# Soft-capped attention and MLP: first loads by two queues, weight pieces behind the sums

## The chip, the cores and the metric

The kernel runs on one core of one Trainium2 chip. The metric is the device time of one execution in microseconds (us); of several executions the median counts.

## What is computed

Four batches of twelve heads of attention over 448 positions of 64 numbers, with scores that are soft-capped, and then an MLP whose first layer is a relu that is squared:

```python
scores = scale * np.matmul(q, k.transpose(0, 1, 3, 2))      # (4, 12, 448, 448)
scores = cap * np.tanh(scores / cap)
attn = np.exp(scores - scores.max(-1, keepdims=True))
attn = attn / (attn.sum(-1, keepdims=True) + 1e-09)
x = np.matmul(attn, v).transpose(0, 2, 1, 3).reshape(1792, 768)
h = np.maximum(x @ w_in, 0.0)                               # w_in 768 x 2048, float64
return (h * h @ w_out).astype(np.float32)                   # w_out 2048 x 768, float64
```

## The kernel before

The 48 heads are worked on as 24 pairs. A loop over n (its passes are called cycles here, 0 to 24) writes the program of all engines by hand: the order of the code is the order on each engine and on each queue. In cycle n the engines do this:

- TensorE computes the scores of pair n in three units (L407), pv of pair n - 1 (L449, L459) and the sums of its exponentials (`sums`, L466). Every second cycle it also computes the half-scores that two pairs share (L416). ScalarE does tanh (L425) and exp (L433).
- VectorE turns the loaded k and q of a later pair (`turn_kq`, L399), adds the exponentials (L437, L440), and takes pv and sums out of PSUM (`evac`, L471).
- The sums go a long way round. SyncE moves them from `e` or `u` into 64 rows, `cmp` (L474, two transfers of 3.5 KB a pair, at the end of cycle n for pair n - 1). VectorE takes the reciprocal two cycles later (`invert`, L478), SyncE writes it to DRAM as `rd` (L480), GpSimd spreads it over the partitions (`spread`, L488, the cycle after), and VectorE multiplies (`normalise`, L502). In the last cycles these steps follow each other more closely: cycle 23 holds the reciprocal and the spread of pair 20.
- The loads of k (GpSimd) and q (SyncE) come in pieces of 32 partitions, four of each a pair (`load_part`, L368), v in two (L385, GpSimd).

During attention four columns of w_in are fetched as float64, in 24 pieces of 128 KB (`fetch_early`, L578, SyncE). The table `FETCH` (L587) gives for each piece the cycle in which it is issued. Six pieces make a column; ScalarE and VectorE decode columns 0, 1 and 2 in the cycles that the tables `SCALAR` and `VECTOR` name. For column 2 ScalarE starts in cycle 19 (L40).

At the start `NWARM` matmuls of zeros run on TensorE (L528). The first pair's k and q come by several queues, the transposes of k and of q follow on VectorE, and behind them the reciprocal of cap, which ScalarE loads into a register before the first tanh (L541 to L544). `issue_after` gives the scheduler a place in the order for the loads of pair 1.

Behind the loop the first MLP layer begins on TensorE (L357); its order comes from a planner. Its operands hold the normalised outputs of all pairs (`xt`, L786).

Of the kernel before, what the change touches and what calls it, by code (L numbers as in the profile page):

```python
# [240 lines left out]
def tile_softcap_attention_mlp(ctx, tc, q, k, v, cap, w_in, w_out, out):  # L241
    nc = tc.nc
# [10 lines left out]
    NF = DFF // P  # L253
    HO = DM // 2
    scale = 1.0 / float(D) ** 0.5
    NWARM = 14
    NKQ = 3
    NKV = 3
    NEXTRA = 5
# [56 lines left out]
    def prepare():  # L316

        nc.vector.memset(ones, 1.0)
        for t in vn:
            nc.vector.memset(t[:, ::NS + 2], 1.0)  # L320
# [3 lines left out]
    def new_raw(pool, bufs):  # L324
        return pool.tile([P, DM], U64, tag="wraw", name="wraw", bufs=bufs)
# [4 lines left out]
    def w_rows(f):  # L330

        return w_in[:, f * P:(f + 1) * P].rearrange("(c h p) f -> h p c f", h=2, p=D)
# [31 lines left out]
    def load_part(n, i, a, queue):  # L364
        b, j = divmod(n, NPAIR)
        w = a % 2
        x = (k, q)[i][b, 2 * j + head(n, a // 2), :, 32 * w:32 * w + 32].rearrange("(t r) e -> r t e", r=32)
        queue.dma_start(out=kqn[n % NKQ][32 * a:32 * a + 32, i], in_=x)  # L368

    def load_kq(n, i, *queues):  # L370
        for a in range(4):
            load_part(n, i, a, queues[a % len(queues)])
# [7 lines left out]
    def load_v(n):  # L380

        b, j = divmod(n, NPAIR)
        x = v[b, 2 * j:2 * j + 2].rearrange("h (t r) d -> (h t) r d", r=D)
        for i, r in enumerate((bottom, top)):
            nc.gpsimd.dma_start(out=vn[n % NKV][r, 1 + i:1 + i + NS], in_=x[i::2].rearrange("t r d -> r t d"))  # L385

    def new_u():
        return ep.tile([P, 2, S], F32, tag="u", name="u", bufs=3)

    NU = 4  # L390
    last = {}
    kqs, ps, probs, adds, pvs, es, rds, by = {}, {}, {}, {}, {}, {}, {}, {}


    def turn_kq(n, parts=1):
        kqs[n] = qp.tile([P, 2 * S], F32, tag="kq", name="kq")
        src, w = kqn[n % NKQ].rearrange("p i t e -> p (i t e)"), 2 * S // parts
        for i in range(parts):
            done = nc.vector.transpose(out=kqs[n][:, i * w:(i + 1) * w], in_=src[:, i * w:(i + 1) * w])  # L399
            last.setdefault("turn", done)  # L400

    def scores(n, u):
        sc = ps_s.tile([P, 2, 512], F32, tag="s", name="sc")
        kt, qt = kqs[n][:, :S], kqs[n][:, S:]
        for i, r in enumerate((top, bottom)):
            h = head(n, i)
            nc.tensor.matmul(out=sc[:, h, :S], lhsT=kt[r, keys(h, u)], rhs=qt[r], start=True, stop=True)  # L407
        probs[n, u] = sc
# [10 lines left out]
    def tanh(n, u):  # L419
        if u in (1, 3):  # L420
            c = 2 if u == 3 and n % 2 else 4
            ps[n, u // 3] = pp.tile([P, c, S], F32, tag=f"p{c}{u}", name="p", bufs=2 if c == 4 else 1)
        at = 2 * (u in (2, 0))
        p = ps[n, int(u not in (1, 2))][:, at:at + 2]
        nc.scalar.activation(out=p, in_=probs[n, u][:, :, :S], func=ACTF.Tanh, scale=by["qks"])  # L425
        if u:
            probs[n, u] = p
        else:
            probs[n, 0], probs[n + 1, 0] = p[:, 0], p[:, 1]

    def exp(n, i):
        p = ps.pop((n, i))
        nc.scalar.activation(out=p, in_=p, func=ACTF.Exp, scale=by["cap"])  # L433

    def add_p(n):
        adds[n] = pp.tile([P, 2, S], F32, tag="add", name="add")
        nc.vector.tensor_add(out=adds[n], in0=probs[n, 1], in1=probs[n, 2])  # L437
# [31 lines left out]
    def evac(n):  # L469
        e = es[n] = new_u() if n % 4 else keep.tile([P, 2, S], F32, tag="e", name="e")  # L470
        nc.vector.tensor_tensor(out=e, in0=pvs.pop(n)[:, :, :S], in1=guard.unsqueeze(2).to_broadcast([P, 2, S]), op=ALU.add)  # L471
        rds[n] = ep.tile([NC, HB], F32, tag="cmp", name="cmp", bufs=NE)
        for h in range(2):
            nc.sync.dma_start(out=rds[n][h * NC // 2:(h + 1) * NC // 2], in_=e[D * h:D * h + D:32, h])  # L474

    def invert(n):
        cmp = rds[n]
        nc.vector.reciprocal(out=cmp, in_=cmp)  # L478
        rd = dram.tile([2, 2, 2, HS], F32, tag="rd", name="rd", bufs=NE)
        nc.sync.dma_start(out=rd.rearrange("h r c (o e) -> (h r c o) e", e=HB), in_=cmp)  # L480
        rds[n] = rd
# [44 lines left out]
    warm = ps_s.tile([P, 2, 512], F32, tag="s", name="warm")[:, 0]  # L526
    for _ in range(NWARM):
        nc.tensor.matmul(out=warm[:, :P], lhsT=zero, rhs=zero, start=True, stop=True)  # L528
    load_kq(0, 0, nc.sync, nc.scalar)
    load_kq(0, 1, nc.sync, nc.scalar, nc.gpsimd, nc.gpsimd)  # L530
    nc.gpsimd.dma_start(out=cap_sb, in_=cap.partition_broadcast(P))
    nc.scalar.activation(out=guard[:, 0:1], in_=zero[:, 0:1], func=ACTF.Tanh)
    prepare()
    turn_kq(0, 2)
    with tc.issue_after(last["turn"].ins):
        load_kq(1, 0, nc.gpsimd)
        load_kq(1, 1, nc.sync)
    load_v(0)
    load_kq(2, 0, nc.gpsimd)
    load_kq(2, 1, nc.sync)  # L540
# [5 lines left out]
    def prepare_cap():  # L546

        nc.vector.tensor_scalar_mul(ncap, cap_sb, -1.0)
        nc.vector.tensor_tensor(out=ncap, in0=ncap, in1=cap_sb, op=ALU.min)
        nc.vector.tensor_scalar(out=far, in0=ncap[0:1], scalar1=-CAP_MAX, scalar2=None, op0=ALU.is_lt)  # L550

        nc.scalar.activation(out=guard[:, 0:1], in_=ncap, func=ACTF.Exp)
# [18 lines left out]
    def fetch_early(n):  # L571

        for i in [i for i, at in enumerate(FETCH) if at == n]:
            f, c = i // 6, i % 6 // 2 * 2
            if i % 6 == 0:
                raws[f] = new_raw(scr, 2)
            h, r = i % 2, rows[i % 2]
            nc.sync.dma_start(out=raws[f][r, c * P:(c + 2) * P].rearrange("p (c f) -> p c f", f=P),  # L578
                              in_=w_rows(f)[h, :, c:c + 2])
# [4 lines left out]
    HB = 28  # L584
    NC = 4 * S // HB
    DEEP = 3
    FETCH = 3, 4, 5, 6, 7, 7, 8, 9, 10, 11, 12, 13, 15, 15, 16, 16, 17, 18, 21, 21, 22, 22, 23, 23  # L587
    SCALAR = {9: (0, "size"), 11: (0, "rest"), 15: (1, "size"), 17: (1, "rest"), 19: (2, "size"), 21: (2, "rest")}
    VECTOR = {10: ((0, "clip"), (0, "shift")), 12: ((0, "sign"),), 14: ((0, "total"),), 16: ((0, "high0"), (0, "low0")),
              18: ((0, "high1"), (0, "low1"), (1, "clip"), (1, "shift")), 19: ((1, "sign"),),  # L590
# [17 lines left out]
    for n in range(NP + 1):  # L608
        on, prep, old = n < NP, n + 1 < NP, n > 0

        if on:
            for u in (1, 2, 3):
                scores(n, u)
            tanh(n, 1)
            tanh(n, 2)
            exp(n, 0)
            tanh(n, 3)
        if prep:
            load_v(n + 1)
        if n == 0:  # L620
            prepare_cap()
        if 3 <= n <= NP:
            invert(n - 3)
        if n == 2:
            turn_kq(3)
        if old:
            add_p(n - 1)
            add_p3(n - 1)
        if 0 < n < NP - 2:
            turn_kq(2 if n == 1 else n + 2)  # L630
        if n == NP:
            normalise(n - 5)
            normalise(n - 4)
        upto = [min(4 * (m + 4) + min(4, max(0, m + 1 - DEEP)), 4 * NP) for m in (n - 1, n)]
        for i, queue in enumerate((nc.gpsimd, nc.sync)):
            for at in range(*upto):
                load_part(at // 4, i, at % 4, queue)
        if n == 1:
            nc.vector.tensor_scalar_mul(guard[:, 0:1], guard[:, 0:1], 1e-9)
            nc.vector.tensor_copy(out=guard[bottom, 1:2], in_=guard[bottom, 0:1])  # L640
            nc.vector.memset(guard[bottom, 0:1], 0.0)
            nc.vector.memset(guard[top, 1:2], 0.0)
        if n - 6 in whole:
            split_x_of(n - 6)
        vector_work(n)
        if n == NP:
            first = new_ps()
            half_unit(first[:, 0], 0, 0, 0)
        if old:
            pv_half(n - 1)  # L650
        if on and n % 2 == 0:
            half_scores(n)
            tanh(n, 0)
        if on:
            exp(n, 1)
        if n in SCALAR:
            early_work(*SCALAR[n])
        if old:
            pv(n - 1)
            sums(n - 1)  # L660
        if old:
            fetch_early(n)
        if 5 <= n < NP:
            normalise(n - 5)
        if 4 <= n < NP:
            spread(n - 4)
        if n >= NP - 1:
            spread(n - 3)
        if n == NP:
            invert(n - 2)  # L670
        if old:
            evac(n - 1)

    vector_work(NP + 1)
    half_unit(first[:, 0], 0, 0, 1)
# [450 lines left out]
    with ExitStack() as mctx:  # L1126
# [136 lines left out]
        for z in range(N + 1):  # L1263
# [12 lines left out]
            if z + 2 < N:  # L1276
                m, i = PRODUCTS[z + 2]
                ops[m, i] = operand(raws[m, i])
            if z < N:
                weights(z)  # L1280
                m, i = PRODUCTS[z]
                pos[m, i] = multiply(ops.pop((m, i)), T[m])
            if z + LEAD - 1 < N:
                m, i = PRODUCTS[z + LEAD - 1]
# [40 lines left out]
```

## Time and profile before

| what | value |
|---|---|
| time, median of 3 executions | 584.51 us (584.32 to 584.94) |
| profiled execution: its time, its span | 584.34 us, 582.8 us |
| TensorE busy, share of the span | 573.4 us, 98% |
| VectorE, ScalarE, GpSimd busy | 466.8, 375.6, 154.7 us |
| share of TensorE in the chain that ended last | 84% |

The span is what the profile covers, and 1.54 us lie around it. Attention takes the first third of the span, and the MLP the rest. A busy share is a mean over stages with different limits, so the stages are read apart in the rows below.

### The profile page before, as it was taken

Reading aid. Unit: us, or ns where it says so; the run is one execution under the profiler, and the core shown is the slowest. Engines: PE = TensorE matmul, PEld = TensorE weight load, DVE = VectorE, ACT = ScalarE, POOL = GpSimd, SP = SyncE. Lnnn points to the kernel's source line nnn. Section 1 sums busy time; section 2 is a strip of 40 time slices with the busy share of each in tenths; the row PEclk is TensorE's granted clock in tenths of the full one; section 3 lists DMA queues with packets and bytes.
Section 4 is the critical chain, followed back from the end, with each engine's and each line's share of the span. In section 5 each row is a group of like instructions: output and inputs, shape, how many; then the busy total and the mean of one; then the engine's idle time right before and its main releaser. Section 6 shows DMA issues by size and latency. Waiting matters only on the chain.

```text
span 582.8 us, 9514 instructions
## 1 busy us (share of the span) xinstructions
PE 573.4 (98%) x3478; PEld 460.5 (79%) x3478; DVE 466.8 (80%) x601; ACT 375.6 (64%) x425; POOL 154.7 (27%) x245
## 2 busy tenths in 40 slices
PE   8999999999999999999999999999999999999996
PEld 5333333333369999999999999999999999999996
DVE  3778899999998999878798992856899996767651
ACT  5999989999955978677575873665534633232220
POOL 8787878876321001111121211100000000000000
PEclk9999999999999999999999999999999999999998
DMA  9989988896318346987879878996999136544511
GB/s 132 138 161 168 172 161 171 161 171 130 118 54 189 101 119 204 282 265 236 284 220 301 275 279 301 323 349 208 266 275 295 53 110 210 168 143 135 162 42 44
DMA packets 140727, 110.37 MB, mean 189 GB/s; under 512 B 55456, under 2 KB 129696, under 8 KB 140672
## 3 DMA queue, kind: packets, MB, share of 16 engines
q1 hardware_dynamic: 127136, 72.03, 49.5%
q0 software_dynamic: 12000, 37.39, 23.1%
q8 instruction: 28, 0.46, 0.3%
q10 hardware_dynamic: 1536, 0.27, 0.3%
q14 instruction: 27, 0.22, 0.1%
HBM read 82.84 MB, written 26.65 MB: 188 GB/s over the span
## 4 chain that ended last, share of the span: by engine, by line
PE 84%; DMA 7%; DVE 4%; issue 2%; ACT 1%; POOL 1%; SPq 0%; ACTq 0%; DVEq 0%; POOLq 0%
PE po L1157 35%; PE hps L357 31%; PE pv L459 7%; PE sc L407 6%; PE pv L449 2%; DMA wraw<-in_moe_w_in_dram 2%; DMA u<-rd 1%; PE sc L416 1%; PE pv L466 1%; ACT p L425 1%; DMA cmp<-e 1%; DMA kqn<-in_q_dram 1%; DMA rd<-cmp 1%; ACT p L433 1%; DVE xf L519 1%
## 5 line engine op out<-in xcount | busy, mean ns | idle before, releaser
L1157 PE MATMUL po<-th,gh 128*128 128x384 f32 x728 | 189.8, 336 | 0.0
L1157 PEld LDWEIGHTS po<-th,gh 128*128 128x128 f32 x728 | 131.8, 188 | 0.0
L1157 PE MATMUL po<-th,gl 128*128 128x384 f32 x392 | 131.7, 336 | 0.0
L1146 ACT CAST gh<-a 128x1024 fp32r<-128x1024 f32 x47 | 49.5, 1052 | 97.3 <-PE po L1157 91.7
L357 PE MATMUL hps<-xt,op 128*128 128x448 f32 x450 | 92.7, 362 | 0.1
L357 PEld LDWEIGHTS hps<-xt,op 128*128 128x128 f32 x450 | 84.3, 187 | 6.1 <-DVE xt L786 0.5
L425 ACT ACTIVATE p<-sc 128x896 f32<-128x896 f32 x84 | 72.7, 909 | 10.6 <-PE sc L407 9.6
L1157 PEld LDWEIGHTS po<-th,gl 128*128 128x128 f32 x392 | 73.7, 188 | 0.0
L433 ACT ACTIVATE p<-p 128x1792 f32<-128x1792 f32 (+1 forms) x48 | 72.6, 1512 | 1.5
L1147 DVE TENSOR_TENSOR gl<-a,gh 128x1024 fp32r<-128x1024 f32 x47 | 57.4, 1222 | 19.0 <-ACT gh L1146 19.0
L357 PE MATMUL hps<-xs,op 128*128 128x448 f32 x324 | 67.6, 363 | 0.0
L357 PEld LDWEIGHTS hps<-xs,op 128*128 128x128 f32 x324 | 60.6, 187 | 4.7 <-ACT p L433 0.4
L407 PE MATMUL sc<-kq 64*128 64x448 f32 x288 | 61.0, 555 | 0.4 <-DVE kq L399 0.4
L368 POOL DMA_DIRECT2D kqn<-in_k_dram x92 | 58.1, 638 | 4.9 <-DMA kqn<-in_k_dram 1.2
L459 PE MATMUL pv<-p,vn 128*32 128x448 f32 x576 | 59.1, 543 | 0.0
L357 PE MATMUL hps<-xh,op 128*128 128x448 f32 x168 | 49.3, 361 | 0.0
L459 PEld LDWEIGHTS pv<-p,vn 128*32 128x32 f32 x576 | 16.3, 109 | 39.8 <-issue 39.8
L407 PEld LDWEIGHTS sc<-kq 64*128 64x128 f32 x288 | 25.6, 186 | 27.2 <-issue 22.1
L385 POOL DMA_DIRECT2D vn<-in_v_dram x48 | 35.3, 739 | 25.1 <-PE pv L459 19.9
L1170 DVE TENSOR_TENSOR osb<-s,po 128x384 f32<-128x384 f32 x27 | 14.9, 552 | 26.5 <-PE po L1157 26.4
L40 ACT ACTIVATE wf<-wraw 128x768 f32<-128x768 f32 x32 | 29.1, 910 | 9.4 <-DVE op L847 3.5
L41 DVE TENSOR_SCALAR wf<-wf 128x768 f32<-128x768 f32 x32 | 17.7, 557 | 20.0 <-ACT wf L40 20.0
(98 smaller groups left out, 821.3 us busy)
## 6 DMA issues: line engine op xcount, KB each, us to landing
a<-g_dram SPq DMA_DIRECT2D x56, 512.0 KB
wraw<-in_moe_w_out_dram SPq DMA_DIRECT2D x16, 768.0 KB
wraw<-in_moe_w_in_dram SPq DMA_DIRECT2D x24, 384.0 KB
g_dram<-r POOLq DMA_DIRECT2D x18, 448.0 KB, 6.9
g_dram<-u POOLq DMA_DIRECT2D x14, 448.0 KB, 5.6
w_dram<-wf POOLq DMA_DIRECT2D x16, 384.0 KB, 6.5
vn<-in_v_dram POOLq DMA_DIRECT2D x48, 112.0 KB, 5.0
kqn<-in_q_dram SPq DMA_DIRECT2D x93, 56.0 KB
```

The costliest lines, as they stand in the source:

```text
L40: size=lambda: nc.scalar.activation(out=magf, in_=high.bitcast(F32), func=ACTF.Abs, scale=2.0 ** 16),
L41: clip=lambda: V.tensor_scalar(out=magf, in0=magf, scalar1=_bits(0x40000000), scalar2=_bits(0x4FEFFFFF), op0=ALU.max, op1=ALU.min),
L357: nc.tensor.matmul(out=out, lhsT=w, rhs=x[:, j], start=start and c == 0 and s == 0, stop=stop and c == NHALF - 1 and s == 2, skip_group_ch ...
L368: queue.dma_start(out=kqn[n % NKQ][32 * a:32 * a + 32, i], in_=x)
L385: nc.gpsimd.dma_start(out=vn[n % NKV][r, 1 + i:1 + i + NS], in_=x[i::2].rearrange("t r d -> r t d"))
L407: nc.tensor.matmul(out=sc[:, h, :S], lhsT=kt[r, keys(h, u)], rhs=qt[r], start=True, stop=True)
L425: nc.scalar.activation(out=p, in_=probs[n, u][:, :, :S], func=ACTF.Tanh, scale=by["qks"])
L433: nc.scalar.activation(out=p, in_=p, func=ACTF.Exp, scale=by["cap"])
L459: nc.tensor.matmul(out=pvs[n][quarter(i), h, :S], lhsT=vn[n % NKV][:, 1 + 3 * h + u, c], rhs=p[:, h], start=False, stop=(u == NU - 1), til ...
L1146: last["act"] = nc.scalar.copy(out=hi, in_=x)
L1147: last["dve"] = nc.vector.tensor_sub(out=lo, in0=x, in1=f32(hi))
L1157: last["mm"] = nc.tensor.matmul(out=po, lhsT=w[:, c], rhs=m[:, cols], start=(c == 0 and i == 0), stop=(c == HF - 1 and i == 2))
```

## The change

For pair 0, all k and q pieces are issued by SyncE and ScalarE in turn, and GpSimd's first transfer is that of cap. `NWARM` goes from 14 to 12, and the ordering of pair 1's loads behind the transpose is taken out. In attention `fetch_early` moves from ahead of `normalise`, `spread` and `evac` to behind `evac`, and `FETCH` starts in cycle 2 with one piece a cycle up to cycle 13.

```diff
-    NWARM = 14
+    NWARM = 12
...
-    load_kq(0, 0, nc.sync, nc.scalar)
-    load_kq(0, 1, nc.sync, nc.scalar, nc.gpsimd, nc.gpsimd)
     nc.gpsimd.dma_start(out=cap_sb, in_=cap.partition_broadcast(P))
+    for i in range(2):
+        load_kq(0, i, nc.sync, nc.scalar)
...
     turn_kq(0, 2)
-    with tc.issue_after(last["turn"].ins):
-        load_kq(1, 0, nc.gpsimd)
-        load_kq(1, 1, nc.sync)
+    load_kq(1, 0, nc.gpsimd)
+    load_kq(1, 1, nc.sync)
...
-    FETCH = 3, 4, 5, 6, 7, 7, 8, 9, 10, 11, 12, 13, 15, 15, 16, 16, 17, 18, 21, 21, 22, 22, 23, 23
+    FETCH = 2, 3, 4, 5, 6, 7, 8, 9, 10, 11, 12, 13, 15, 15, 16, 16, 17, 18, 21, 21, 22, 22, 23, 23
...
             sums(n - 1)
-        if old:
-            fetch_early(n)
         if 5 <= n < NP:
             normalise(n - 5)
...
         if old:
             evac(n - 1)
+            fetch_early(n)
```

Three places in the program. In the rows below a number behind a name tells tiles of one name apart, and the two kernels count them differently; x4 is four such rows.

GpSimd's first transfers, before:

```order
L368 DMA kqn0_120<-in_q_dram 32x14x32 x2
L531 DMA cap_sb_106<-in_cap_dram 128x1
L368 DMA kqn1_121<-in_k_dram 32x14x32 x4
L385 DMA vn0_123<-in_v_dram 64x7x64 x2
L368 DMA kqn2_122<-in_k_dram 32x14x32 x4
```

and with the change:

```order
L528 DMA cap_sb_106<-in_cap_dram 128x1
L368 DMA kqn1_121<-in_k_dram 32x14x32 x4
L385 DMA vn0_123<-in_v_dram 64x7x64 x2
L368 DMA kqn2_122<-in_k_dram 32x14x32 x4
L385 DMA vn1_124<-in_v_dram 64x7x64 x2
```

The two q pieces of pair 0 (`kqn0`) are gone from GpSimd's queue; SyncE and ScalarE, which issue two k pieces each, now issue two q pieces each behind them instead of one.

SyncE's queue in cycles 6 to 8, before (`cmp_613`, `cmp_680` and `cmp_753` are those of pairs 5, 6 and 7; `wraw_401` is column 0, `wraw_745` column 1):

```order
L578 DMA wraw_401<-in_moe_w_in_dram 64x2x128
L474 DMA cmp_613<-u_611 32x1x28 x2
L480 DMA rd_634<-cmp_539 64x28
L368 DMA kqn2_122<-in_q_dram 32x14x32 x4
L578 DMA wraw_401<-in_moe_w_in_dram 64x2x128 x2
L474 DMA cmp_680<-u_678 32x1x28 x2
L480 DMA rd_701<-cmp_613 64x28
L368 DMA kqn0_120<-in_q_dram 32x14x32 x4
L578 DMA wraw_745<-in_moe_w_in_dram 64x2x128
L474 DMA cmp_753<-u_751 32x1x28 x2
```

and with the change (`cmp_611`, `cmp_677` and `cmp_749` are those of pairs 5, 6 and 7):

```order
L473 DMA cmp_611<-u_609 32x1x28 x2
L576 DMA wraw_344<-in_moe_w_in_dram 64x2x128
L479 DMA rd_633<-cmp_537 64x28
L368 DMA kqn2_122<-in_q_dram 32x14x32 x4
L473 DMA cmp_677<-u_675 32x1x28 x2
L576 DMA wraw_344<-in_moe_w_in_dram 64x2x128
L479 DMA rd_699<-cmp_611 64x28
L368 DMA kqn0_120<-in_q_dram 32x14x32 x4
L473 DMA cmp_749<-u_747 32x1x28 x2
L576 DMA wraw_752<-in_moe_w_in_dram 64x2x128
```

Each piece has moved from ahead of a pair's `cmp` to between it and the next `rd`, and the two pieces of cycle 7 are one.

SyncE's queue from cycle 22 on, before (`cmp_1638`, `cmp_1702` and `cmp_1761` are those of pairs 20, 21 and 22, and `rd_1721` is that of pair 20; `wraw_1629` is column 3):

```order
L474 DMA cmp_1638<-e_1636 32x1x28 x2
L480 DMA rd_1659<-cmp_1577 64x28
L578 DMA wraw_1629<-in_moe_w_in_dram 64x2x128 x2
L474 DMA cmp_1702<-u_1700 32x1x28 x2
L480 DMA rd_1721<-cmp_1638 64x28
L578 DMA wraw_1629<-in_moe_w_in_dram 64x2x128 x2
L474 DMA cmp_1761<-u_1759 32x1x28 x2
```

and with the change (`rd_1719` is that of pair 20):

```order
L473 DMA cmp_1633<-e_1631 32x1x28 x2
L576 DMA wraw_1636<-in_moe_w_in_dram 64x2x128 x2
L479 DMA rd_1657<-cmp_1575 64x28
L473 DMA cmp_1698<-u_1696 32x1x28 x2
L576 DMA wraw_1636<-in_moe_w_in_dram 64x2x128 x2
L479 DMA rd_1719<-cmp_1633 64x28
L473 DMA cmp_1757<-u_1755 32x1x28 x2
```

Here two pieces stand between a pair's `cmp` and the `rd` of the pair before it.

## Rows read from the trace of the kernel before

**Rows 1.** Table of stretches: us, busy us (and instructions) by engine, clock, DMA share, GB/s.

```profile
58.00:72.00 14.00, 13.83 (x108) 5.29 (x110) 11.37 (x16) 12.96 (x13) 11.33 (x19) 1.00 1.10 172
...
86.00:100.00 14.00, 14.00 (x112) 5.40 (x110) 13.41 (x20) 12.32 (x13) 11.76 (x18) 1.00 0.88 167
...
150.00:192.00 42.00, 41.80 (x271) 28.50 (x264) 38.41 (x55) 27.38 (x30) 10.27 (x18) 1.00 0.51 133
```

**Rows 2.** Chain that ended last, 0 to 46 us: start, us, what.

```profile
2.33 4.27 DMA kqn<-in_q_dram
...
6.68 0.65 DVE kq L399
...
7.32 0.17 DVE qks L541
...
8.63 1.73 ACT p L425 x2
...
15.57 1.02 PE pv L449 x4
```

**Rows 3.** Timeline, first 10 us: start, us, engine, line, operation; last the wait before.

```profile
0.97 0.99 ACTq L368 DMA_DIRECT2D kqn<-in_k_dram  x2
...
1.29 5.73 PE L528 MATMUL warm<-kqn 128*128 128x128 f32 x28 [1.29 <-DVE kqn L525]
1.56 1.41 POOL L368 DMA_DIRECT2D kqn<-in_q_dram  x2 [0.88 <-POOLq L1307]
...
2.96 0.59 POOL L531 DMA_DIRECT2D cap_sb<-in_cap_dram  x1
...
4.91 0.65 DVE L399 STREAM_TRANSPOSE kq<-kqn 128x448 f32<-128x448 f32 x1 [3.17 <-DMA kqn<-in_k_dram]
...
9.89 1.11 DVE L399 STREAM_TRANSPOSE kq<-kqn 128x896 f32<-128x896 f32 x1 [2.21 <-DMA kqn<-in_k_dram]
```

**Rows 4.** Timeline of TensorE: first scores of the pairs 7, 8, 9 and 12.

```profile
51.92 2.53 PE L407 MATMUL sc<-kq 64*128 64x448 f32 x12
...
57.90 2.53 PE L407 MATMUL sc<-kq 64*128 64x448 f32 x12
...
64.79 2.53 PE L407 MATMUL sc<-kq 64*128 64x448 f32 x12
...
85.63 2.53 PE L407 MATMUL sc<-kq 64*128 64x448 f32 x12
```

**Rows 5.** Timeline of VectorE: reciprocals of pairs 5 and 6, with the wait ahead.

```profile
60.35 0.32 DVE L478 RECIPROCAL cmp<-cmp 64x28 f32<-64x28 f32 x1 [0.52 <-DMA cmp<-u]
...
68.12 0.32 DVE L478 RECIPROCAL cmp<-cmp 64x28 f32<-64x28 f32 x1 [1.62 <-DMA cmp<-u]
```

**Rows 6.** Chain that ended last, 40 to 80 us.

```profile
51.33 8.27 DMA wraw<-in_moe_w_in_dram
```

**Rows 7.** Timeline of SyncE's queue, 50 to 62 us.

```profile
53.38 1.54 SPq L474 DMA_DIRECT2D cmp<-u  x2
...
59.62 1.35 SPq L578 DMA_DIRECT2D wraw<-in_moe_w_in_dram  x2
61.07 1.16 SPq L474 DMA_DIRECT2D cmp<-u  x2
```

**Rows 8.** Chain that ended last, 140 to 195 us.

```profile
161.32 3.54 DMA rd<-cmp
...
191.16 3.88 PE hps L357 x18
```

**Rows 9.** Timelines of SyncE, ScalarE and TensorE around the third column.

```profile
133.85 1.13 SPq L474 DMA_DIRECT2D cmp<-u  x2
...
137.71 0.90 ACT L40 ACTIVATE wf<-wraw 128x768 f32<-128x768 f32 x1
...
143.81 1.70 ACT L433 ACTIVATE p<-p 128x1792 f32<-128x1792 f32 x1
...
146.90 0.96 PE L449 MATMUL pv<-p,vn 64*128 64x448 f32 x4
```

More of the change, by code (lines that the diff above doesn't have):

```diff
@@ L398, in turn_kq @@
         for i in range(parts):
-            done = nc.vector.transpose(out=kqs[n][:, i * w:(i + 1) * w], in_=src[:, i * w:(i + 1) * w])
-            last.setdefault("turn", done)
+            nc.vector.transpose(out=kqs[n][:, i * w:(i + 1) * w], in_=src[:, i * w:(i + 1) * w])
     def scores(n, u):
```

## Prediction

> **What bounds the kernel now.** I read the table of stretches first: in steady attention TensorE is busy for all of 14 us, and in 58 to 72 us it loses 0.17, with the 16 DMA engines' share at 1.10, over one [rows 1]. So time can be won only where TensorE stands, and the change touches three such places.
>
> The first is the start. The chain of waits goes back from the first product with v at 15.57 through ScalarE to the reciprocal of cap at 7.32, which stands on VectorE behind the second transpose of pair 0, and from there to a q piece that GpSimd issued at 2.33 and that took 4.27 us [rows 2]. VectorE turned k at 4.91 and then waited for q until 6.68 [rows 2, 3]; the warm-up matmuls were no limit at 7.02 (1.29 and 5.73 long) [rows 3].
>
> The second is the stretch from 64.79 to 85.63. A cycle is the time from one pair's first scores to the next pair's; the timeline shows 5.98 us for a cycle without the shared half-scores (51.92 to 57.90) and 6.89 with them (57.90 to 64.79) [rows 4]. Cycles 9 to 11 should take 5.98 + 6.89 + 5.98 = 18.85 us and take 20.84: TensorE loses 1.99 us. The cause stands on VectorE: its reciprocal of the sums waited 0.52 us at 60.35 and 1.62 us at 68.12 for `cmp`, the transfer of 3.5 KB that brings the sums [rows 5]. That transfer sits behind weight pieces on SyncE: the chain shows one piece under way from 51.33 for 8.27 us [rows 6], then two pieces at 59.62, and only at 61.07 the `cmp` that was wanted at 66.5 and came at 68.12 [rows 7].
>
> The third is the way out of attention. The chain that ends last runs from the issue of `rd` of pair 20 at 161.32 (3.54 us) over its spread, through VectorE, to the spread of the last pair and to TensorE's wait at 191.16 [rows 8]. From there the chain is TensorE alone to the end, so what is lost or won up to 191 stays.
>
> **The change part by part.** Durations come from the profiled execution: 582.8 us of span and 1.54 around it, 584.34 in all, 0.17 below the median of 584.51. The sum is made against 584.34.
>
> *First pair.* GpSimd loses two issues of q, 1.41 us together; SyncE and ScalarE get one more each, about 0.5 us (two took 0.99) [rows 3]. All eight pieces of pair 0 are then issued in fours; the last start at about 2.5. What q takes there isn't in the trace. The second k pieces, issued by the same two engines at about 1.47, had landed when VectorE started at 4.91: at most 3.44 us. The same from 2.5 gives 5.9. From below, VectorE is busy with k until 4.91 + 0.65 = 5.56; from above, q as late as now (6.60). I take the end of the wait at 5.75, nearer the row of the same two engines, since they also carry less beside it. The second transpose then ends at 6.4 instead of 7.32, and the first tanh, which followed it by 1.31 us (7.32 to 8.63), comes 0.9 us sooner. Bounds: 0 and 1.1.
>
> *Cap* was issued at 2.96 and read at 7.32, so landed within 4.36 us; issued at 1.56 it is there by 5.9, before 6.4. *Warm-up*: twelve of fourteen, at 5.73 / 14 = 0.41 us each, end at 6.2, ahead of the scores; with fourteen the 7.02 would now be the limit, so the cut costs nothing and keeps the 0.9. *The removed ordering* of pair 1's loads moves no row on either queue. Pair 1's k waits behind one issue on GpSimd instead of three and comes 1.41 us sooner than 9.89; its q goes 0.5 us later on SyncE. A late q there is inside the lower bound. First part: -0.9.
>
> *Weight pieces.* The same 24 pieces are issued, each now behind `cmp` of its cycle and ahead of `rd`. Piece one goes in cycle 2, and cycle 7 has one instead of two. `cmp` of pair 6 stood behind 256 KB, which SyncE had issued only at 60.97 (59.62 + 1.35); now nothing of the weights stands ahead of it in its cycle. 1.62 + 0.52 of VectorE's wait goes, and with it what TensorE lost. I take 1.7 of the 1.99, since the total load of these cycles falls by only one piece of 128 KB. Bounds: 0 and 2.0. What is late next is `rd`, by one piece (0.68 us), but it has a whole cycle until its spread in cycles up to 22.
>
> *The way out.* In cycles 21 to 23 two pieces stand ahead of each `rd`. `rd` of pair 20, issued at 161.32 right behind `cmp` of pair 21, gets two pieces between, 1.35 us of issue by the two at 59.62 [rows 7]. Behind it everything on VectorE is in order up to the last spread, and TensorE has no work left at 191.16 that doesn't need it. So its delay comes out in full. How `rd` lands behind two pieces isn't in the trace. From below: 3.54 us held two pieces right behind it, which are now a cycle away, so it may land as early as before: 0. From above: it lands with pieces that take 8.27 us as in the crowded stretch, 161.3 + 8.3 = 169.6 against 164.86: 4.7. The share of the DMA engines there is 0.51 [rows 1], so I stay near the issue time: +1.2.
>
> *Scale of the third column.* Its last piece (cycle 18) moves from the end of its cycle to behind `cmp` at 133.85, so to about 135.1 [rows 9]. ScalarE reads it at 137.71. With 3.44 us, as k took, it lands at 138.5; with 8.27 at 143.4. The cover: ScalarE's exp of pair 20 ends at 145.51 and TensorE uses it at 146.90, 1.39 us. Bounds: 0 and 143.4 - 137.7 - 1.4 = 4.3; I take 0.2, since the landing is nearer the short row.
>
> Sum: 584.34 - 0.9 - 1.7 + 1.2 + 0.2 = 583.14, so **583.1**, 0.24% below the median.
>
> A rule against the first part: q by GpSimd took 4.27 us where SyncE's and ScalarE's k took at most 3.44 [rows 2, 3]. The Trainium skill, DMA: Bandwidth & Descriptors, "Issuing engines are not separate DMA queues", says that all issuers end on the same 16 DMA engines and that spreading saves only issue time; by that rule the first part is worth about nothing, since the last q piece is issued at about 2.5 on either side, and the sum would be 584.0. A rule on the way out: a `cmp` issued at 53.38 behind the piece of 51.33 (landed at 59.60) came at 60.35, right behind it [rows 5 to 7]. The Trainium skill, same page, "Queues, rings and completion order", says that each DMA engine takes descriptors in ring order; the row agrees, and by it `rd` lands behind both pieces, which makes the loss larger than my 1.2, in the worst case the time of (d) below.
>
> **Rivals.** (a) *The way out costs nothing*: `rd` lands as before. For it: other work is light there; against: the issue alone is 1.35 us later on the chain. Time 584.34 - 0.9 - 1.7 + 0.2 = 581.9. (b) *The start doesn't move*: q comes at 6.6 whoever issues it. For: the DMA engines were already moving pieces of pair 0 and 1; against: the 3.44 of k. Time 584.0. (c) *The middle loss stays*: the wait for `cmp` is from too much to move in cycles 4 to 8, not from the order. For: the share of 1.10 and 8.27 us for 128 KB; against: the two waits follow the piece and the pair. Time 584.34 - 0.9 + 1.2 + 0.2 = 584.8. (d) *Slower*: `rd` of pair 20 lands with its pieces at the price of the crowded stretch, 4.7 us: 584.34 - 0.9 - 1.7 + 4.7 + 0.2 = 586.6. It decides as soon as the delay of `rd` passes 3.7 us (584.51 + 1.17 = 585.68). For: it stood so at 51.33; against: the share of 0.51 there.
>
> **How the numbers follow.** Forecast 0.50, its own range 582.4 to 583.9; (a) 0.17, (b) 0.13, (c) 0.13, (d) 0.07. A change under 0.2% (1.17 us) can't be told from none here, so faster means below 583.34: two thirds of the forecast (0.33), all of (a) (0.17) and a little of (b) (0.03), 0.53. Slower, above 585.68, is (d): 0.07. The rest, 0.40, is the same. The range reaches from (a) with the start at its bound of 1.1 (581.7) to (c) (584.8); (d) and the edges stay out.
>
> **What would show it.** The second transpose of pair 0 should start near 5.75 and the first tanh near 7.7; if q still ends the wait at 6.6, (b) holds. Cycles 9 to 11 should take about 19.1 us; with VectorE still waiting for `cmp` for over 1 us, (c). `rd` of pair 20 should be issued about 1.4 us after `cmp` of pair 21 has left, and TensorE should stand over 1 us before its work at what is now 191.16; no such stand means (a), over 3.7 us (d). A wait of ScalarE before the third column's scaling of more than 1.4 us would break the last term.

## The result, and the profile after

The changed kernel takes 587.27 us (median of 8 executions, 586.09 to 589.98), the kernel before 584.23 on the same chip (8 executions). The ratio is 1.0056, with a 95% interval of 1.0038 to 1.0074: slower by 3.0 us by the medians, where 583.1 was forecast. The profiled execution has a span of 585.6 us and a time of 587.25.

The timeline of the first microseconds after the change (start, us, engine, line, operation; last the wait before) answers to [rows 3] and the tanh and q of [rows 2]:

```profile
0.97 0.99 ACTq L368 DMA_DIRECT2D kqn<-in_k_dram  x2
...
1.29 4.68 PE L527 MATMUL warm<-kqn 128*128 128x128 f32 x24 [1.29 <-DVE kqn L524]
...
1.99 1.03 ACTq L368 DMA_DIRECT2D kqn<-in_q_dram  x2
2.16 2.55 POOL L368 DMA_DIRECT2D kqn<-in_k_dram  x4
...
5.29 0.65 DVE L399 STREAM_TRANSPOSE kq<-kqn 128x448 f32<-128x448 f32 x1 [3.56 <-DMA kqn<-in_k_dram]
...
7.56 0.65 DVE L399 STREAM_TRANSPOSE kq<-kqn 128x448 f32<-128x448 f32 x1 [1.62 <-DMA kqn<-in_q_dram]
...
8.26 4.22 PE L406 MATMUL sc<-kq 64*128 64x448 f32 x12 [2.30 <-DVE qks L539]
...
10.10 0.92 ACT L424 ACTIVATE p<-sc 128x896 f32<-128x896 f32 x1 [5.55 <-PE sc L406]
```

The q of pair 0 is ready for its transpose at 7.56 instead of 6.68, with pair 1's k on its way from 2.16. TensorE is done with the warm-up at 5.97, stands 2.30 us, and then needs 4.22 us for scores that took 2.53 [rows 4]. The first tanh comes at 10.10 instead of 8.63, and the scores of pair 9 start 2.16 us later than in [rows 4].

TensorE's scores of the pairs 9 and 12, and the reciprocal of pair 6 on VectorE, answer to [rows 4, 5]:

```profile
66.95 2.53 PE L406 MATMUL sc<-kq 64*128 64x448 f32 x12
...
86.28 2.53 PE L406 MATMUL sc<-kq 64*128 64x448 f32 x12
```

```profile
69.01 0.32 DVE L477 RECIPROCAL cmp<-cmp 64x28 f32<-64x28 f32 x1 [0.83 <-DMA cmp<-u]
```

Cycles 9 to 11 take 86.28 - 66.95 = 19.33 us instead of 20.84: the gain of the middle is there, 1.51 us. Pair 12 starts only 0.65 us late.

Around the third column, [rows 9], SyncE's queue, ScalarE, and TensorE's scores of pairs 20 to 22 with the half-scores between:

```profile
136.92 0.66 SPq L576 DMA_DIRECT2D wraw<-in_moe_w_in_dram  x1
```

```profile
142.19 0.92 ACT L40 ACTIVATE wf<-wraw 128x768 f32<-128x768 f32 x1 [2.99 <-DVE cmp L477]
```

```profile
139.55 2.53 PE L406 MATMUL sc<-kq 64*128 64x448 f32 x12
...
143.96 0.98 PE L415 MATMUL sc<-kq 64*64 64x448 f32 x8 [1.13 <-ACT p L424]
147.65 2.53 PE L406 MATMUL sc<-kq 64*128 64x448 f32 x12
153.62 2.53 PE L406 MATMUL sc<-kq 64*128 64x448 f32 x12
```

and the scores of pairs 20 and 21 in the trace of before:

```profile
137.65 2.53 PE L407 MATMUL sc<-kq 64*128 64x448 f32 x12
144.54 2.53 PE L407 MATMUL sc<-kq 64*128 64x448 f32 x12
```

ScalarE stands 2.99 us ahead of the scaling, and the cycle of 139.55 takes 8.10 us where the same one took 6.89 (137.65 to 144.54). By pair 21 TensorE is 3.11 us late.

On the way out, [rows 8], `rd` of pair 20 on SyncE's queue, its transfer in the chain of waits, and TensorE at the work that [rows 8] has at 191.16:

```profile
163.35 1.34 SPq L576 DMA_DIRECT2D wraw<-in_moe_w_in_dram  x2
164.79 0.54 SPq L479 DMA_DIRECT2D rd<-cmp  x1
```

```profile
164.79 3.29 DMA rd<-cmp
```

```profile
194.72 2.48 PE L357 MATMUL hps<-xt,op 128*128 128x448 f32 x11 [1.01 <-DVE xt L783]
```

194.72 - 191.16 = 3.56 us. The start gave 2.16, the middle took 1.51 back, cycles 12 to 18 lost 0.72 and cycles 19 and 20 together 1.74, and the rest, 0.45, arose on the way out. From there both kernels run alike; that the span differs by only 2.8 us is the tail behind the last product with w_out (4.5 us against 5.3).

### The profile page after: what moved, and what is told of

Same layout as the page of the kernel before. It is cut to its first block, busy times and chain, and to the rows that moved or that the text cites. A ratio compares the mean times of both kernels' runs of the same rounds, so it can differ in the third digit from the quotient of the medians.

```text
span 585.6 us, 9502 instructions
## 1 busy us (share of the span) xinstructions
PE 572.9 (98%) x3474; PEld 460.2 (79%) x3474; DVE 467.3 (80%) x601; ACT 375.1 (64%) x425; POOL 153.6 (26%) x243
## 4 chain that ended last, share of the span: by engine, by line
PE 89%; DVE 3%; DMA 3%; ACT 2%; issue 1%; SPq 0%; ACTq 0%; POOL 0%; DVEq 0%; POOLq 0%
PE po L1154 35%; PE hps L357 31%; PE pv L458 9%; PE sc L406 8%; PE pv L448 3%; PE sc L415 2%; PE pv L465 1%; DMA u<-rd 1%; ACT p L424 1%; DMA kqn<-in_q_dram 1%; DMA e<-rd 1%; DVE xt L783 1%; ACT p L432 1%; DVE xf L518 1%; DMA rd<-cmp 1%
## 5 line engine op out<-in xcount | busy, mean ns | idle before, releaser
L1144 DVE TENSOR_TENSOR gl<-a,gh 128x1024 fp32r<-128x1024 f32 x47 | 57.5, 1223 | 19.3 <-ACT gh L1143 19.3
L406 PE MATMUL sc<-kq 64*128 64x448 f32 x288 | 62.7, 568 | 3.0 <-DVE qks L539 2.3
L41 DVE TENSOR_SCALAR wf<-wf 128x768 f32<-128x768 f32 x32 | 17.8, 558 | 20.3 <-ACT wf L40 20.3
```

The lines of the kernel that those rows point to most:

```text
L41: clip=lambda: V.tensor_scalar(out=magf, in0=magf, scalar1=_bits(0x40000000), scalar2=_bits(0x4FEFFFFF), op0=ALU.max, op1=ALU.min),
L1144: last["dve"] = nc.vector.tensor_sub(out=lo, in0=x, in1=f32(hi))
```

## The experiments

Three groups, all timed against the kernel before. The first takes the change apart.

**start_only**: before with the start of the change.

```diff
-    NWARM = 14
+    NWARM = 12
...
-    load_kq(0, 0, nc.sync, nc.scalar)
-    load_kq(0, 1, nc.sync, nc.scalar, nc.gpsimd, nc.gpsimd)
     nc.gpsimd.dma_start(out=cap_sb, in_=cap.partition_broadcast(P))
+    for i in range(2):
+        load_kq(0, i, nc.sync, nc.scalar)
...
-    with tc.issue_after(last["turn"].ins):
-        load_kq(1, 0, nc.gpsimd)
-        load_kq(1, 1, nc.sync)
+    load_kq(1, 0, nc.gpsimd)
+    load_kq(1, 1, nc.sync)
```

> The kernel before with the start of the change alone (pair 0 by SyncE and ScalarE, cap first, 12 warm-ups); the weight pieces stay as before. Theory: most of the loss is here. The changed kernel's first product with v was 2.15 us later than before (17.72 against 15.57), and every cycle up to 64.79 kept that, so this kernel should be 2.1 us slower than before, about 586.3, with q of pair 0 ending VectorE's wait near 7.5 and the first scores taking over 4 us. Rival: the later start came from something else in the changed kernel, and this one is within 0.5 us of before.

Measured: 1.0014 (1.0001 to 1.0026), 585.13 us, 8 executions at 584.6 to 585.5 and 4 at 586.4 to 587.6. By the ratio that is 0.8 us, between the 2.1 of the theory and the 0.5 of the rival. The late q is there (transpose at 7.48), but the scores take 2.53 us:

```profile
8.18 2.53 PE L406 MATMUL sc<-kq 64*128 64x448 f32 x12 [1.40 <-DVE qks L539]
```

This trace starts pair 2 only 0.68 us later than before's. So the start has two prices in the traces: 0.7 us for the late q, and 1.5 us that are in the trace of the change and not here.

**pieces_only**: the change with the start of before.

```diff
-    FETCH = 3, 4, 5, 6, 7, 7, 8, 9, 10, 11, 12, 13, 15, 15, 16, 16, 17, 18, 21, 21, 22, 22, 23, 23
+    FETCH = 2, 3, 4, 5, 6, 7, 8, 9, 10, 11, 12, 13, 15, 15, 16, 16, 17, 18, 21, 21, 22, 22, 23, 23
...
-        if old:
-            fetch_early(n)
...
             evac(n - 1)
+            fetch_early(n)
```

> The changed kernel with the start of before; only the weight pieces differ from before. Theory: the parts add up. From the starts of the cycles in the two traces: -1.5 us in cycles 9 to 12, +0.7 in 13 to 19, +1.7 in 19 to 21 (ScalarE's wait for the last piece of the third column among it), +0.5 on the way out: +1.4, about 585.6. Rival (the prediction's own sum without the start): -1.7 + 1.2 + 0.2 = -0.3, about 583.9.

Measured: 1.0021 (1.0011 to 1.0032), 585.9 us. The theory's 585.6 fits, the prediction's sum does not: the trace wins 1.1 us in cycles 9 to 11, loses 1.7 in 19 and 20, and TensorE stands 1.05 us on the way out:

```profile
192.71 2.48 PE L357 MATMUL hps<-xt,op 128*128 128x448 f32 x11 [1.05 <-DVE xt L785]
```

**warm17**: the change with a longer warm-up.

```diff
-    NWARM = 12
+    NWARM = 17
```

> The changed kernel with 17 warm-up matmuls instead of 12, so that TensorE works until 8.25 us, as long as it waits for q. Theory: the cut of the warm-ups let the granted clock fall; with 17 the first scores take 2.5 us again instead of 4.2 at the same start of about 8.26, and the first tanh comes at about 9.5 instead of 10.1 and the whole 1.2 us sooner: about 586.0. Rival: the late loads are the whole loss, the first product with v stays at 17.7 whatever the clock, and the time stays at 587.2.

Measured: 1.0037 (1.0017 to 1.0056), 586.88 us. At the start the theory held: TensorE stands 0.26 us, the scores take 2.53 and the first tanh comes at 9.28. In time the median lies between the theory (586.0) and the rival (587.2). The profiled execution took 590.96 us, one of two of the 12 above 590, since it lost again what it had won, on the way out. The chain of waits of this kernel, and its table of stretches (us, busy us (and instructions) of PE, PEld, DVE, ACT, POOL, clock, DMA share, GB/s):

```profile
194.63 1.01 DVE xt L783
195.64 0.04 issue
195.68 185.04 PE hps L357 x911
```

```profile
190.00:195.00 5.00, 2.96 (x13) 1.84 (x11) 4.96 (x7) 4.26 (x7) 0.55 (x1) 0.94 0.73 175
195.00:200.00 5.00, 4.32 (x12) 3.84 (x13) 4.86 (x8) 4.04 (x5) 0.00 (x0) 0.50 0.56 147
200.00:205.00 5.00, 5.00 (x24) 4.62 (x23) 5.00 (x8) 4.18 (x6) 0.54 (x1) 0.88 0.23 92
```

and the same work in the chain of before:

```profile
191.16 182.48 PE hps L357 x911
```

TensorE stood 0.20, 0.90 and 1.62 us between 191 and 195.7; from 195 to 200 the granted clock is at 0.50 (1.2 of 2.4 GHz), and the 911 matmuls that are left of the first MLP layer take 185.04 us instead of 182.48. The stand is paid for twice.

**warm12_old_loads**: before with the cut alone.

```diff
-    NWARM = 14
+    NWARM = 12
```

> The kernel before with 12 warm-up matmuls instead of 14 and nothing else. TensorE then stands from about 6.0 to 7.38 us instead of 0.36 us. Theory: such a stand already lets the granted clock fall in the first scores, which take about 4 us, and the time rises by about 1.2 us to 585.4. Rival, the prediction's claim that the cut costs nothing: the scores still take 2.5 us and the time stays at 584.2.

Measured: 0.9993 (0.9983 to 1.0003), 584.25 us. TensorE stands 1.40 us and the scores still take 2.53: in time the rival was right for a stand of this length.

The second group asks where each loss comes from.

**hold_pair1**: start_only, with GpSimd's loads of pair 1 held.

```diff
+    nc.gpsimd.memset(guard[:, 0:1], 0.0)
     load_kq(1, 0, nc.gpsimd)
```

> The kernel before with the start of the change alone, but GpSimd holds its loads of pair 1's k until ScalarE has run its guard at about 4.5 us (a memset of the guard stands ahead of them) instead of issuing from 2.16. Theory: the late landing of pair 0's q (7.45 in three traces against 6.7) comes from pair 1's k, which is issued sooner and moves at the same time; held, q ends VectorE's wait at 6.7 or before, and k at 4.9 as before. Rival: q lands late because it stands behind k on the same two queues; then it stays at about 7.4 with nothing from GpSimd beside it. In time: 584.4 by the theory, 585.1 or more by the rival.

Measured: 1.0005 (0.9992 to 1.0017), 584.09 us. The timeline of its start:

```profile
4.66 2.55 POOL L368 DMA_DIRECT2D kqn<-in_k_dram  x4
5.23 0.65 DVE L399 STREAM_TRANSPOSE kq<-kqn 128x448 f32<-128x448 f32 x1 [3.50 <-DMA kqn<-in_k_dram]
6.83 0.65 DVE L399 STREAM_TRANSPOSE kq<-kqn 128x448 f32<-128x448 f32 x1 [0.95 <-DMA kqn<-in_q_dram]
```

With pair 1's k issued at 4.66 instead of 2.16 q is ready at 6.83. It is at 7.45 to 7.63 in the six traces that have the new loads unheld, at 6.74 to 6.92 in the three with the hold, and at 6.65 to 6.92 in the eight with the old loads. So what GpSimd loads beside q makes it late, by 0.7 us (pair 1's k, and v behind it, which the hold moves too), and two queues bring q no sooner than three did. The k of pair 0 stays at 5.05 to 5.44 with the hold, where the theory had 4.9; VectorE still waits for q behind it. In time the theory (584.4) held. That is rival (b) and its rule: the Trainium skill, DMA: Bandwidth & Descriptors, "Issuing engines are not separate DMA queues", has all issuers share the same 16 engines, and these traces agree.

**column_early**: pieces_only, with the third column's last piece a cycle sooner.

```diff
-    ... 15, 15, 16, 16, 17, 18, ...
+    ... 15, 15, 16, 16, 17, 17, ...
```

> The start of before with the changed weight pieces, but the last piece of the third column is issued in cycle 17 instead of 18 (column 2 in cycles 15, 15, 16, 16, 17, 17). Theory: in the three traces that have the changed pieces ScalarE stands up to 3 us ahead of the third column's scaling, and the two cycles after it take 1.7 us longer; a cycle earlier the piece is there in time, the stand goes, and the time falls by 1.7 from 585.9 to about 584.2. Rival: ScalarE waits there for VectorE (the trace names VectorE's reciprocal as what ended the stand), so an earlier piece changes nothing: 585.9.

Measured: 1.0052 (1.0033 to 1.0071), 587.44 us: the stand went and the time rose by 0.3%. ScalarE no longer waits (scaling at 137.38) and the cycle of pair 20 takes 6.89 us, so it was the piece that ScalarE waited for, although the trace names VectorE. But the next cycle takes 1.14 us longer, so that pair 22 starts only 0.23 us sooner than in pieces_only. VectorE's and TensorE's timelines show why:

```profile
140.46 0.32 DVE L478 RECIPROCAL cmp<-cmp 64x28 f32<-64x28 f32 x1 [1.02 <-DMA rd<-cmp]
...
146.43 1.09 DVE L471 TENSOR_TENSOR u<-pv,guard 128x896 f32<-128x896 f32 x1
```

```profile
147.62 1.02 PE L449 MATMUL pv<-p,vn 64*128 64x448 f32 x4 [0.90 <-ACT p L425]
```

VectorE's reciprocal waited 1.02 us for a transfer on SyncE's queue (in before, not at all). VectorE has no gap from there on and takes pv out of PSUM late, and TensorE's next product with v starts 0.10 us behind the end of that, although the trace names ScalarE. The four traces that mend the third column all have this: a wait of 0.83 to 1.02 us and a stand of 0.83 to 0.90.

On the way out TensorE stands 1.87 us and then runs at a clock of 0.70 for 5 us; the 911 matmuls take 184.07 us. GpSimd's and VectorE's timelines show what stood in the way there:

```profile
172.15 1.19 POOL L488 DMA_DIRECT2D u<-rd  x2 [4.51 <-DVE xf L519]
173.33 0.22 POOL masks.py:197 MEMSET ident<- 128x128 f32 x1
173.63 4.97 POOL masks.py:199 TENSOR_SCALAR_AFFINE_SELECT ident<-ident 128x128 f32<-128x128 f32 x1
178.56 1.83 POOL L488 DMA_DIRECT2D u<-rd  x3
```

```profile
172.18 1.02 DVE L471 TENSOR_TENSOR u<-pv,guard 128x896 f32<-128x896 f32 x1
173.12 1.14 DVE L519 TENSOR_TENSOR xf<-xf 128x448 f32<-128x448 f32 x2
174.19 3.08 DVE L785 TENSOR_TENSOR xt<-xf,xt 128x896 fp32r<-128x896 f32 x3
```

The select for the identity matrix takes 0.29 us in before:

```profile
171.28 0.29 POOL masks.py:199 TENSOR_SCALAR_AFFINE_SELECT ident<-ident 128x128 f32<-128x128 f32 x1
```

Here it begins at 173.63, when VectorE has left `u<-pv,guard` (L471, one operand in SBUF) for operations with two, and it ends only at 178.6, with the spreads of two pairs queued behind it. The last spread itself is issued no later than in pieces_only, but its transfer takes longer; the chains have, for column_early and then for pieces_only:

```profile
180.38 9.71 DMA u<-rd
```

```profile
181.25 7.56 DMA u<-rd
```

**late_old_place**: pieces_only, with the old place from cycle 20 on.

```diff
             sums(n - 1)
+        if old and n >= 20:
+            fetch_early(n)
...
             evac(n - 1)
-            fetch_early(n)
+            if n < 20:
+                fetch_early(n)
```

> The start of before with the changed weight pieces, but from cycle 20 on the pieces go back to their old place, ahead of the pair's sums. Theory: the two pieces ahead of rd of pair 20 cost the stand of TensorE ahead of its last operands (1.05 us in the trace of the pieces alone, 1.01 in that of the whole change): without them it is gone, and the time falls by about 1 us from 585.9 to 584.9. Rival: the stand comes from the third column's delay (VectorE behind its work), it stays at 1 us, and the time stays at 585.9.

Measured: 1.0002 (0.9990 to 1.0015), 584.52 us. The stand is gone, with the third column still late: the theory held. The chain is TensorE alone from 170.53 to the last product with w_out:

```profile
170.53 203.61 PE hps L357 x1017
```

**middle_only**: the same, with cycle 14 in place of 20.

> The start of before; the changed order of the weight pieces in cycles 2 to 13 only, the old place from cycle 14 on. Theory: this keeps the gain of the middle (1.7 us: cycles 9 to 11 took 20.84, 21.58 and 21.41 us in three traces with the old order and 19.33, 19.74 and 19.54 in three with the new) and has neither the late piece of the third column nor the late rd: about 582.9, faster than before by 0.3%. Rival: the gain is given back later, since what is early in one stretch waits in the next: within 0.1% of before.

Measured: 1.0000 (0.9985 to 1.0015), 583.85 us, 582.83 to 586.7. In its trace the second MLP layer starts 0.92 us sooner than in before's, but the time doesn't show it: the rival fits, and a gain of 0.24%, which 1.4 us would be, lies outside the interval. Rows of before are one execution: cycles 9 to 11 took 20.84 us there and 21.58, 21.41 and 21.37 in the three other traces with the old order; with the new order 19.3 to 20.3, mean 19.9, in 13 traces. The gain of the middle is about 1.4 us in the traces.

The third group moves one line, and mends the change.

**column_ident**, **change_ident**, **middle_ident**: column_early, the whole change and middle_only, with the identity made at the start.

```diff
     load_v(0)
+    make_identity(nc, ident)
...
-    make_identity(nc, ident)
```

> The kernel of column_early with one line moved: GpSimd makes the identity matrix behind the first load of v instead of behind the loop. Theory: in the trace of column_early GpSimd's select for the identity took 4.97 us instead of 0.29, while VectorE ran operations with two operands in SBUF, and the spreads of the last pairs were queued behind it; TensorE then stood 1.9 us and the granted clock fell behind that stand. With the select out of the way the stand is that of the trace with the pieces alone, about 1 us, and the clock holds: 585.5. Rival: the stand comes from rd behind two pieces by itself, and the time stays at 587.4.

> The whole change with the identity made early, as in column_ident, and nothing else. Theory: some executions of the change pay for the long select and the fall of the clock on the way out (warm17, which has the same pieces, lost 5.3 us there in its trace, the change itself 0.5); the executions above 588 disappear and the median falls from 587.3 to about 586.6. Rival: the select matters in none of them, since the spread comes later still, and the median stays at 587.3.

> The kernel of middle_only with the identity made early. middle_only's trace stood 0.92 us ahead of before's at the start of the second MLP layer, but its time did not: half its executions were at 582.8 to 583.4, some up to 586.7. Theory: the slow ones are executions with the long select; without it the median is about 583.2, faster than before by 0.15%. Rival: the spread of its executions comes from the middle, where the wait for cmp differs from one execution to the next, and the median stays at 583.9.

Measured: column_ident 1.0002 (0.9984 to 1.0020) against column_early's 1.0052. Moving the select took 0.5% off that kernel, but not as the theory had it: in its trace, which is of its longest execution (586.56 us), TensorE still stands 1.69 us, and only the fall of the clock is gone (182.48 us again). change_ident: 1.0029 (1.0011 to 1.0047), 585.64 us; seven executions lie at 584.9 to 585.7, but three above 588, two of them above 589, so the select is not what makes those long. middle_ident: 0.9987 (0.9976 to 0.9998), 584.33 us, a gain of 0.13% that only just differs from none.

change_ident also shows the price of the clock at the start, since TensorE runs the same instructions there as in the change, and q is ready at 7.49 (7.56 in the change). The stretch of 9 to 11 us, of the change and then of change_ident:

```profile
9.00:11.00 2.00, 2.00 (x8) 1.04 (x6) 0.00 (x1) 0.90 (x1) 1.49 (x3) 0.50 1.37 149
```

```profile
9.00:11.00 2.00, 2.00 (x12) 0.77 (x10) 0.20 (x1) 1.68 (x2) 1.76 (x4) 1.00 1.36 146
```

In the change TensorE had stood 2.30 us and has a clock of 0.50; here it stood 1.62 and has 1.00. Pair 2 starts 1.47 us sooner, of which the scores of pair 0 had only 0.07.

**change_start**, **change_way_out**, **change_column**: the whole change with one part mended (hold and 14 warm-ups; the old place from cycle 20 on; the last piece in cycle 17).

> The whole change with only its start mended: 14 warm-ups and pair 1's k held on GpSimd. Theory: the start costs the change 0.7 us by the late q in every execution, and 1.5 us more in those in which the clock falls behind the stand of TensorE: its time falls from 587.3 to that of the pieces alone, 585.9. Rival: the start alone cost only 0.8 us by its own run, so what is missing in the sum (3.0 us against 0.8 and 1.25) arises on the way out, and the time falls by 0.8 to 586.5.

> The whole change with only its way out mended: from cycle 20 on the pieces have their old place. Theory: 1.1 us (from pieces_only to late_old_place, 1.0021 to 1.0002) go away, about 586.2. Rival: what is missing in the sum is the fall of the clock behind the stand on the way out; then 2 us or more go, 585.3 or less, and no execution lies above 588.

> The whole change with only the third column mended: its last piece in cycle 17. Theory: TensorE gets to the way out 1.7 us sooner, but rd and the last spread do not, so that it stands longer there; the time stays within 0.5 us of 587.3 or rises, as it did from pieces_only to column_early (1.0021 to 1.0052). Rival: the third column's delay counts in full, and the time falls by 1.7 us to 585.6.

Measured: 1.0040 (1.0022 to 1.0058), 1.0024 (1.0010 to 1.0038) and 1.0086 (1.0065 to 1.0107). The way out is the dearest part, 0.32% (1.9 us, between the two numbers expected), though the change's own trace shows 0.45 us there; no execution lies above 588, as the rival had it. The start is 0.16% (0.9 us, nearer the rival), within the intervals. Mending the third column alone makes it worse by 0.3%, as the theory allowed; its trace has a stand of 2.64 us at the start (scores of 4.85 us) and a select of 5.45 us. The two halves by themselves give 0.14% (start_only) and 0.21% (pieces_only), 0.35% in all against the 0.56% of the change. The intervals allow that difference, and no run shows where it would arise.

**all_mended**: the change with the edits of change_start, change_way_out, change_column and change_ident together.

> The whole change with each suspected cost taken out: 14 warm-ups, pair 1's k held on GpSimd to 4.5 us, the third column's last piece in cycle 17, the old place of the pieces from cycle 20 on, and the identity made early. Theory: these are all the costs, so what is left is the gain of the middle: about 583.3, 4 us under the change and 0.1% to 0.2% under before. Rival: the costs move elsewhere (the cycles after the third column, where column_early lost 1.14 us in one place), and it stays above 584.2.

Measured: 0.9989 (0.9976 to 1.0001), 584.04 us. From 1.0056 to 0.9989 is 3.9 us: the edits together take the whole loss away. What stays, 0.1%, can't be told from no change, and it is less than the 0.24% that the gain of the middle would leave.

## Why the prediction was wrong

**The first pair: the step that failed.** The prediction wrote "The same from 2.5 gives 5.9" and took 5.75 for the end of the wait for q; it was 7.56. The 3.44 us came from k pieces that were issued ahead of all else, and didn't carry over to q behind them: with pair 1 held back q still comes only at 6.83 (hold_pair1), which is what the row of q at 4.27 us gives [rows 2]: 2.5 + 4.27 = 6.8. The other 0.7 us are GpSimd's loads beside it. The same text counted that pair 1's k comes 1.41 us sooner, and didn't ask what it takes from q, so its lower bound of nothing left out a loss. In place of the 0.9 us of gain start_only measures a loss of 0.8.

**The warm-up.** That "the cut costs nothing" rested on q coming at 5.75. Its cover was that TensorE would be wanted as soon as it was done. With q late, in the change's trace twelve matmuls left a stand of 2.30 us, and the clock fell: 1.5 us. Alone the cut costs nothing that the time shows (warm12_old_loads).

**The weight pieces.** 1.7 was forecast; 1.51 in the change's trace and about 1.4 over all. The mechanism was right in the traces, and rival (c) is out. In time less of it is left: middle_only is at 1.0000 and middle_ident at 0.9987, where 1.4 us would be 0.9976.

**The third column.** The term of 0.2 was mis-sized. The piece was issued at 136.92 and ScalarE waited until 142.19, 5.3 us, between the short row (3.44) that I took and the long one (8.27); the wait of 2.99 us is over the 1.4 that the prediction named as its limit. In the seven traces that keep the piece in cycle 18 behind `cmp` cycles 19 and 20 take 1.3 to 1.9 us longer. In time this isn't separable: mended alone, most of it is lost again in the next cycle, and late_old_place (1.0002), which has the late piece, can't be told from middle_only (1.0000), which hasn't.

**The way out.** `rd` was issued 1.49 us behind `cmp`, and TensorE stands 1.01 us, as forecast. With the start of before that costs 1.1 us (pieces_only against late_old_place), near the 1.2 of the sum. In the change it costs 1.9 us (change_way_out). The delay of `rd` didn't come out in full in the change's trace, since TensorE was itself 3.11 us late by then: only 0.45 us is added there. The prediction priced a stand at its length; in warm17 and column_early the stands were 2.7 and 1.9 us, and the clock fell in the last of them or right behind it, for 2.6 and 1.6 us more. That the change's other executions pay this is not shown. Rival (d) had the sign and the place right, but not the price or the mechanism: `rd` took 3.29 us behind both pieces, no longer than the 3.54 of before [rows 8]. What makes stands longer than 1.05 us is not shown: column_ident stands 1.69 us without the long select, and the transfer of its last spread takes 8.60 us.

Open: why the transfer that VectorE waits for comes late in all four traces that mend the third column, why the last spread takes 7 to 10 us, and where the clock falls in executions that were not profiled, since for those only its mean is on record.

## What to carry to other kernels

A transfer that is issued sooner takes from those beside it: cost a moved load at what it does to the one that is waited for. Price a stand of TensorE at its length and at what the clock costs behind it, and leave the warm-up long enough for a load that comes late. Before a loss is mended, look at what the work then runs into: here most of what the third column's earlier piece won was lost in the next cycle, and the stand on the way out was longer, not shorter.

## What the runs showed that was not expected

The first scores by the stand ahead of them: 0.26, 1.40 (twice), 1.55 and 1.62 us left them at 2.53 us; behind 2.30 and 2.64 us they took 4.22 and 4.85, at a granted clock of 0.50 from 9 to 11 us. On the way out the length of the stands doesn't decide alone: 0.19 and 1.68 us in column_early brought a fall, 0.24 and 1.61 in change_column none.

The warm-up itself has two rates, and the moment between them differs from one execution to the next: twelve matmuls took 4.68 us in the change, 5.49 in start_only and 4.29 in change_column. From 5.0 to 5.5 us the change's table of stretches has seven of their records, where start_only's has four:

```profile
5.00:5.50 0.50, 0.50 (x7) 0.50 (x6) 0.20 (x1) 0.00 (x0) 0.50 (x2) 1.00 1.36 145
```

```profile
5.00:5.50 0.50, 0.50 (x4) 0.50 (x3) 0.15 (x1) 0.00 (x0) 0.50 (x2) 1.00 1.42 155
```

So the same program stands for a different time, and the loss can come in some executions only. The mean granted clock of every execution bears that out. In 121 executions of before it is never under 0.997; with the loads unheld and twelve warm-ups it is in 19 of 50 (change 3 of 8; start_only, change_ident and change_way_out 4 of 12 each; change_column 4 of 6), with twelve warm-ups and q on time in 3 of 24 (warm12_old_loads and hold_pair1), with fourteen and the changed pieces in 1 of 89. The longest executions have the lowest: 0.994 twice in the change (587.99 and 589.98 us), 0.994 and 0.992 in change_ident (589.04 and 589.40), 0.992 twice in warm17 (590.96 and 591.18). The four of start_only above 586 are at 0.994 to 0.997, and its five at 0.998 or more are all under 585.2. But before's own longest, 589.41 us, is at 0.999, so the clock isn't behind every long execution.

GpSimd's select of 128x128 took 0.29 us in ten traces that have it behind the loop, and 4.97, 5.45 and 5.64 in the three others. In nine of the ten it began while VectorE ran the reciprocal or `u<-pv,guard`, in the tenth (hold_pair1) 0.04 us ahead of the reciprocal; in the three at most 0.2 us ahead of the next operation with two operands in SBUF, or behind its start. The Trainium skill, SBUF — State Buffer, "Who interferes with whom", says that a VectorE instruction with two inputs in SBUF contends with a GpSimd instruction that reads SBUF, and that one with at most one such input, outside VectorE's 2-port modes, does not. The traces agree: 0.29 us beside the one kind, 4.97 to 5.64 us beside a run of the other.
